# Loading one row of wo per partition in pieces of 69, 48 and 11 partitions, and pairing the exp and transpose tiles, in a cached-attention decode kernel

## The chip, the cores and the metric

The kernel runs on one core of a Trainium2 chip. Of its engines the text names PE (matrix multiplications; PEld is its loading of weights), DVE (vectors), ACT (functions such as exp), POOL and SP, whose queue issues the large loads; 16 DMA engines move the data. A load has landed when its bytes are in the core's memory of 128 partitions. The metric is device microseconds of one execution, lower is better; quoted times are medians over several executions. Executions of one kernel agree within 0.15%, so differences of half a per cent can be told, and "faster" or "slower" needs 2%.

## The reference, cut to what matters

One token goes through two branches that a sigmoid gate mixes. The attention branch has 32 query heads, 4 key/value heads and a cache of 65536 positions, and ends in the projection with `wo`. Inputs are bf16.

```python
q = (x @ wq).reshape(B, Sq, 32, 128).transpose(0, 2, 1, 3)
scores = einsum('bhqd,bhkd->bhqk', q, repeat(k_cache, 8)) * 128 ** -0.5
o = einsum('bhqk,bhkd->bhqd', softmax(scores), repeat(v_cache, 8))
a = o.transpose(0, 2, 1, 3).reshape(B, Sq, 4096) @ wo       # wo is 4096 x 1024
# ... the other branch b: an input projection, gelu, layernorm, an output projection
return g * a + (1 - g) * b
```

The two caches are 64 MB each (4 x 65536 x 128 x 2 bytes), and with the weights 162 MB have to be read once. `wo` is 8 MB of that and is read last.

## The kernel before: the parts that the argument touches

Everything large goes through one buffer `kv` of four slots (4 MB each over 128 partitions), by loads issued on the SP queue. A K tile is transposed on DVE, multiplied on PE, and its scores are copied to an `sc` tile. After the four tiles of a key/value head, `stats` takes the maximum, runs exp on ACT and transposes the result on DVE for the V matmuls:

```python
    def stats(g):
        # ... maximum over the head's four tiles, into nb
        lss[g] = wk.tile([P, NT], FP32, name="ls")
        for j in range(NT):
            nc.scalar.activation(out=sct[g, j][:], in_=sct[g, j][:], func=ACT.Exp, scale=SCALE,
                                 bias=nb[:, 0:1], accum_out=lss[g][:, j:j + 1])
            ptt[g, j] = ptp.tile([P, CC, B], BF16, name="pt")
            nc.vector.transpose(out=ptt[g, j][:].rearrange("p c x -> p (c x)"),
                                in_=sct[g, j][:])
```

The last loads are those of `wo`. A partition holds 32 rows of it (2 KB each): 16 in the first load, then 8, 4, 2, 1 and 1, so that little is left to compute after the last landing:

```python
    wo_view = A_wo.rearrange("(p c) n -> p c n", c=OC)
    c0 = 0
    for at, split in enumerate(WO_SPLIT):              # ((16,), (8, 4, 2, 1, 1))
        for n in split:
            t = load(wo_view[:, c0:c0 + n, :], (n, D), at + c0 % (OC // 2) * D / (CT * P))
            project(t, n, oa, c0, last=(c0 + n == OC))
            c0 += n
```

Of the kernel before, what the change touches and what calls it, by code (L numbers as in the profile page):

```python
# [8 lines left out]
FP32 = mybir.dt.float32  # L9
BF16 = mybir.dt.bfloat16  # L10
I32 = mybir.dt.int32
ACT = mybir.ActivationFunctionType
ALU = mybir.AluOpType
AX = mybir.AxisListType

P = 128
CT = 128
NKV = 4
B = 32
NB = P // B  # L20
VC = 4
CC = CT // VC
ZN = 448
HN = 512
WO_SPLIT = ((16,), (8, 4, 2, 1, 1))


@with_exitstack
def kernel(
# [15 lines left out]
    nc = tc.nc  # L45

    _, _, D = A_x.shape
    _, G, S, DH = A_k_cache.shape
# [7 lines left out]
    OC = HD // P  # L56
    QD = P // H
    NT = S // (P * CT)
# [3 lines left out]
    SCALE = float(DH) ** -0.5  # L62
# [5 lines left out]
    wk = ctx.enter_context(tc.tile_pool(name="wk", bufs=2))  # L68
    big = ctx.enter_context(tc.tile_pool(name="big", bufs=1))
    ktp = ctx.enter_context(tc.tile_pool(name="ktp", bufs=3))  # L70
    scp = ctx.enter_context(tc.tile_pool(name="scp", bufs=NT + 1))
    ptp = ctx.enter_context(tc.tile_pool(name="ptp", bufs=NT + 2))
    pss = ctx.enter_context(tc.tile_pool(name="pss", bufs=2, space=bass.MemoryType.PSUM))
    psm = ctx.enter_context(tc.tile_pool(name="psm", bufs=1, space=bass.MemoryType.PSUM))
    pso = ctx.enter_context(tc.tile_pool(name="pso", bufs=1, space=bass.MemoryType.PSUM))
# [81 lines left out]
    kv = big.tile([P, NKV * CT * P], BF16, name="kv")  # L157

    def load(src, shape, at):
        n = 1  # L160
        for s in shape:
            n *= s
        v = kv[:, int(at * CT * P):int(at * CT * P) + n]
        if len(shape) == 2:
            v = v.rearrange("p (a b) -> p a b", b=shape[1])
        ins = nc.sync.dma_start(out=v, in_=src)  # L166
        if not first_load:
            first_load.append(ins.ins.name)
        return v

    def load_kv(src, g, j, at, n=1):
# [62 lines left out]
    for t in range(2):  # L234
        nc.vector.tensor_tensor(
            out=xm[:, t], in0=xb_ps[:, t * P:(t + 1) * P].rearrange("p (i c) -> p c i", c=KC),
# [51 lines left out]
    for hf in range(2):  # L288
        nc.vector.tensor_tensor(  # L289
            out=zm[:, hf], in0=z_ps[:, hf * HN:hf * HN + ZN].rearrange("p (j c) -> p j c", c=FC),  # L290
# [3 lines left out]
                            in_=zm.rearrange("p h j c -> p h c j"), axis=AX.X, op=ALU.add)  # L294
# [44 lines left out]
    for k in range(NHB):  # L339
# [3 lines left out]
                                                                   j=B, e=2),  # L343
# [29 lines left out]
    late = []  # L373
    sct, ptt, mxs, lss, o_ps = {}, {}, {}, {}, {}

    def k_tile(g, j, kn):
        kb = kn.bitcast(I32)
        n = CC * DH // 2
        s_ps = pss.tile([P, 2 * HN], FP32, name="s_ps", tag="s")
        for v in range(VC):  # L380
            kt = ktp.tile([P, CC * DH], BF16, name="kt")
            nc.vector.transpose(out=kt[:].bitcast(I32), in_=kb[:, v * n:(v + 1) * n])  # L382
            while late:
                nc.vector.reduce_max(**late.pop())  # L384
            kx = kt[:].rearrange("p (c h k e) -> p h e c k", h=2, k=B, e=2)
            for b in range(BP):
                for k in range(2):
                    ins = nc.tensor.matmul(  # L388
                        s_ps[:, k * HN:(k + 1) * HN],
                        lhsT=wt[g % 2][:, v, b].rearrange("p a v h -> p (a v h)"),  # L390
                        rhs=kx[:, b // 2, b % 2, k * CC // 2:(k + 1) * CC // 2, :],
                        start=(v == 0 and b == 0), stop=(v == VC - 1 and b == BP - 1),
                        skip_group_check=True)
                    if k > 0:
                        same_weights(ins)
        if j == 0:
            mxs[g] = wk.tile([P, NT], FP32, name="mx")
        sct[g, j] = scp.tile([P, CC * B], BF16, name="sc")
        nc.scalar.copy(out=sct[g, j][:], in_=s_ps[:])  # L399
        late.append(dict(out=mxs[g][:, j:j + 1], in_=sct[g, j][:], axis=AX.X))  # L400

    def stats(g):
        nc.vector.reduce_max(**late.pop())  # L403
        m1 = wk.tile([P, 1], FP32, name="m1")
        nc.vector.reduce_max(out=m1[:], in_=mxs[g][:], axis=AX.X)  # L405
        mt_ps = psm.tile([1, P], FP32, name="mt_ps", tag="m")
        nc.tensor.transpose(mt_ps[:], m1[:], ident_f[:])  # L407
        gm = wk.tile([1, REP], FP32, name="gm")
        nc.vector.tensor_reduce(out=gm[:], in_=mt_ps[:].rearrange("p (a h) -> p h a", h=REP),
                                axis=AX.X, op=ALU.max)  # L410
        gr = wk.tile([1, P // REP, REP], FP32, name="gr")
        nc.vector.tensor_copy(out=gr[:], in_=gm[:].unsqueeze(1).to_broadcast([1, P // REP, REP]))
        nb_ps = psm.tile([P, 1], FP32, name="nb_ps", tag="m")
        nc.tensor.matmul(nb_ps[:], lhsT=gr[:].rearrange("p a h -> p (a h)"),
                         rhs=ones_f[0:1, 0:1], start=True, stop=True)
        nb = wk.tile([P, 1], FP32, name="nb")
        nc.vector.tensor_scalar(out=nb[:], in0=nb_ps[:], scalar1=-SCALE, scalar2=None,  # L417
                                op0=ALU.mult)
        lss[g] = wk.tile([P, NT], FP32, name="ls")
        for j in range(NT):  # L420
            nc.scalar.activation(out=sct[g, j][:], in_=sct[g, j][:], func=ACT.Exp, scale=SCALE,  # L421
                                 bias=nb[:, 0:1], accum_out=lss[g][:, j:j + 1])
            ptt[g, j] = ptp.tile([P, CC, B], BF16, name="pt")
            nc.vector.transpose(out=ptt[g, j][:].rearrange("p c x -> p (c x)"),  # L424
                                in_=sct[g, j][:])

    def v_tile(g, j, vt):
        if j == 0:
            o_ps[g] = pso.tile([P, 2, VC * DH], FP32, name="o_ps")
        vx = vt.rearrange("p (v c d) -> p c v d", v=VC, d=DH)  # L430
        for u in range(CC // 2):
            hs = slice(u % 2 * P // 2, (u % 2 + 1) * P // 2)
            for e in range(2):
                ins = nc.tensor.matmul(  # L434
                    o_ps[g][hs, e, :],
                    lhsT=ptt[g, j][:, 2 * u:2 * u + 2, :].rearrange("p c x -> p (c x)"),
                    rhs=vx[:, 2 * u + e], start=(j == 0 and u < 2),
                    stop=(j == NT - 1 and u >= CC // 2 - 2), skip_group_check=True)
                if e > 0:
                    same_weights(ins)  # L440

    def head_out(g):
        gs = slice(g * B, (g + 1) * B)
        om8 = big.tile([P, 2 * VC, DH], FP32, name="om8")
        nc.vector.tensor_tensor(  # L445
            out=om8[:], in0=o_ps[g][:].rearrange("p e (v d) -> p (e v) d", d=DH),
            in1=own_8[:].unsqueeze(2).to_broadcast([P, 2 * VC, DH]), op=ALU.mult)
        o_sb = wk.tile([P, DH], FP32, name="o_sb")
        nc.vector.tensor_reduce(out=o_sb[:], in_=om8[:].rearrange("p x d -> p d x"), axis=AX.X,  # L449
                                op=ALU.add)  # L450
        om_ps = psm.tile([P, DH + NT], FP32, name="om_ps", tag="m")
        hs = hsel[:].rearrange("p h q -> p (h q)")
        nc.tensor.matmul(om_ps[gs, DH:], lhsT=hs, rhs=lss[g][:], start=True, stop=True,
                         skip_group_check=True)
        nc.tensor.matmul(om_ps[gs, :DH], lhsT=hs, rhs=o_sb[:], start=True, stop=True,  # L455
                         skip_group_check=True)
        rl = wk.tile([P, 2], FP32, name="rl")
        nc.vector.reduce_sum(out=rl[gs, 0:1], in_=om_ps[gs, DH:], axis=AX.X)
        nc.vector.reciprocal(out=rl[gs, 1:2], in_=rl[gs, 0:1])
        om = wk.tile([P, QD, OC], FP32, name="om")  # L460
        nc.vector.tensor_tensor(
            out=om[gs], in0=om_ps[gs, :DH].rearrange("p (q c) -> p q c", c=OC),
            in1=own_q[gs, :].unsqueeze(2).to_broadcast([B, QD, OC]), op=ALU.mult)
        osum = wk.tile([P, OC], FP32, name="osum")
        nc.vector.tensor_reduce(out=osum[gs, :], in_=om[gs].rearrange("p q c -> p c q"),
                                axis=AX.X, op=ALU.add)
        nc.vector.tensor_scalar(out=oa[gs, :], in0=osum[gs, :], scalar1=rl[gs, 1:2],
                                scalar2=gate[gs, :], op0=ALU.mult, op1=ALU.mult)
# [38 lines left out]
    c0 = 0  # L507
    for at, split in enumerate(WO_SPLIT):
        for n in split:
            t = load(wo_view[:, c0:c0 + n, :], (n, D), at + c0 % (OC // 2) * D / (CT * P))  # L510
            project(t, n, oa, c0, last=(c0 + n == OC))
            c0 += n
    out_sb = const.tile([P, NO], BF16, name="out_sb")
# [45 lines left out]
```

## Time and profile before

| | before |
|---|---|
| median time | 383.88 us (383.83 to 383.91, 3 runs) |
| span of the profiled run | 382.1 us |
| rate of the big loads, from 50 to 370 us | 4 MB every 9.72 us (431 GB/s) |
| last landing of the last V load, of the last `wo` load | 359.68 us, 379.41 us |

The first lines of the page give each engine's busy time and its share of the span; part 3 gives, for each DMA queue, packets, megabytes and the share of the 16 DMA engines' time:

```profile
PE 236.9 (62%) x1372; PEld 60.0 (16%) x796; DVE 218.7 (57%) x211; ACT 39.6 (10%) x55; POOL 4.4 (1%) x10
...
DMA  9999999999999999999999999899999999999995
...
q1 hardware_dynamic: 5188, 162.01, 98.7%
q8 instruction: 8, 0.13, 0.1%
q14 instruction: 3, 0.02, 0.0%
```

The big loads keep the 16 DMA engines busy for 98.7% of the span, and no compute engine passes 62%. So the time is the time of the loads, plus a few microseconds at both ends. Part 3 shows two more queues, with eleven packets: they are instruction fetches.

The end of the chain of waits (start, duration, what):

```profile
340.38 9.32 PE o_ps L434 x64
...
351.51 27.90 DMA kv<-in_A_wo_dram
379.41 0.04 issue
379.45 0.32 PE out_ps L476 x4
```

After 351.51 us there is nothing but waiting for `wo`, and what comes after the landing is short. The exp and the transposes, in the groups part, take a few per cent of two engines that have time to spare (busy us, mean ns | idle before them and its cause):

```profile
L424 DVE STREAM_TRANSPOSE pt<-sc 128x1024 bf16<-128x1024 bf16 x16 | 18.6, 1217 | 6.8 <-ACT sc L421 6.8
...
L421 ACT ACTIVATE sc<-sc,nb 128x1024 bf16<-128x1024 bf16 x16 | 18.2, 1136 | 9.6 <-DVE nb L417 9.6
```

For each load of 128 partitions the trace shows 16 landings, and the page counts 16 DMA engines; a landing is taken as that of one engine's share. For the last `wo` load they were (us):

```
377.34 377.38 377.46 377.55 377.59 377.70 378.21 378.76 378.91 379.01 379.07 379.11 379.13 379.19 379.20 379.41
```

The engines do not end together: six end within 0.4 us, and nine end 1.4 to 2.1 us after the first. The lag has a visible cause. The trace has eight instruction fetches of 16 KB (1.02 to 1.10 us each) and three of 8 KB (0.31 to 0.33 us), and from a fetch on one engine lands later in every load: by about 1.55 us (1.53 to 1.56) after each 16 KB fetch whose engine can be followed, and by 0.7 or 0.97 us after an 8 KB fetch. So a fetch is taken to run on one of the same engines. The spread at the end is what the change is after.

### The profile page before, as it was taken

The page shows a single profiled execution, that of the slowest core. Times are in us where ns is not written, and L with a number is a line of the kernel's source. Part 1 is how long each engine was busy: PE and PEld are TensorE (multiplying, and loading weights), DVE is VectorE, ACT ScalarE, POOL GpSimd, SP SyncE. Part 2 cuts the span into 40 slices and gives each one's busy share as a digit, 9 for nine tenths or more (in the row PEclk, how much of TensorE's full clock was granted, in tenths as well). Part 3 has the DMA queues.
Part 4 walks back from the last instruction along what each step waited for, and adds up shares of the span by engine and source line. Part 5 has one row for each costly group of instructions (what it writes and reads, how often), then busy time and mean ns, then how long its engine had stood idle before and what let it go on. Part 6 is the DMA issues. An engine that isn't in the chain of part 4 may idle for free.

```text
span 382.1 us, 2629 instructions
## 1 busy us (share of the span) xinstructions
PE 236.9 (62%) x1372; PEld 60.0 (16%) x796; DVE 218.7 (57%) x211; ACT 39.6 (10%) x55; POOL 4.4 (1%) x10
## 2 busy tenths in 40 slices
PE   0433457777257966774879485548776964539355
PEld 0110011111111211121112011211111111112123
DVE  4241477997498379555971586659804976400040
ACT  1010001110601101140011011400110105000000
POOL 4000000000000000000000000000000000000000
PEclk9999999998859899867689789897888996959768
DMA  9999999999999999999999999899999999999995
GB/s 379 442 422 418 427 433 439 439 436 428 427 432 429 425 437 453 432 418 418 461 439 394 439 478 439 379 422 463 425 413 432 460 426 425 432 412 427 439 412 221
DMA packets 5239, 162.17 MB, mean 424 GB/s; under 512 B 616, under 2 KB 620, under 8 KB 1004
## 3 DMA queue, kind: packets, MB, share of 16 engines
q1 hardware_dynamic: 5188, 162.01, 98.7%
q8 instruction: 8, 0.13, 0.1%
q14 instruction: 3, 0.02, 0.0%
q10 hardware_dynamic: 40, 0.01, 0.0%
HBM read 162.01 MB, written 0.00 MB: 424 GB/s over the span
## 4 chain that ended last, share of the span: by engine, by line
DMA 57%; PE 22%; DVE 15%; issue 3%; ACT 2%; SPq 0%; DVEq 0%; ACTq 0%
DMA kv<-in_A_v_cache_dram 31%; DMA kv<-in_A_k_cache_dram 14%; DVE kt L382 12%; PE o_ps L434 11%; PE s_ps L388 10%; DMA kv<-in_A_wo_dram 7%; DMA kv<-in_B_w_in_dram 5%; DVE pt L424 1%; ACT sc L399 1%; PE z_ps L275 1%; DVE o_sb L449 0%; SPq L166 0%; ACT L421 0%; ACT sc L421 0%; DVE om L445 0%
## 5 line engine op out<-in xcount | busy, mean ns | idle before, releaser
L388 PE MATMUL s_ps<-kt,wt 128*128 128x512 bf16 x512 | 138.4, 428 | 63.5 <-DVE kt L382 63.3
L382 DVE STREAM_TRANSPOSE kt<-kv 128x2048 int32<-128x2048 int32 x64 | 142.7, 2280 | 39.5 <-DMA kv<-in_A_k_cache_dram 39.5
L434 PE MATMUL o_ps<-kv,pt 128*64 128x512 bf16 x512 | 69.3, 437 | 22.4 <-DMA kv<-in_A_v_cache_dram 22.4
L388 PEld LDWEIGHTS <-wt 128*128 128x128 bf16 x256 | 27.1, 106 | 175.9 <-issue 138.1
L399 ACT CAST sc<-s_ps 128x1024 bf16<-128x1024 f32 x16 | 16.2, 1013 | 245.9 <-PE s_ps L388 245.9
L445 DVE TENSOR_TENSOR om<-o_ps,own 128x1024 f32<-128x1024 f32 x4 | 4.9, 1225 | 46.0 <-PE o_ps L434 46.0
L434 PEld LDWEIGHTS <-pt 128*64 128x64 bf16 x256 | 19.5, 125 | 69.9 <-issue 65.0
L424 DVE STREAM_TRANSPOSE pt<-sc 128x1024 bf16<-128x1024 bf16 x16 | 18.6, 1217 | 6.8 <-ACT sc L421 6.8
L384 DVE TENSOR_REDUCE mx<-sc 128x1 f32<-128x1024 bf16 x12 | 14.5, 1209 | 9.5 <-ACT sc L399 9.4
L421 ACT ACTIVATE sc<-sc,nb 128x1024 bf16<-128x1024 bf16 x16 | 18.2, 1136 | 9.6 <-DVE nb L417 9.6
L403 DVE TENSOR_REDUCE mx<-sc 128x1 f32<-128x1024 bf16 x4 | 4.9, 1220 | 13.6 <-ACT sc L399 13.6
L275 PE MATMUL q_ps<-kv,xT 128*32 128x512 bf16 x64 | 7.2, 630 | 7.3 <-DMA kv<-in_A_wq_dram 7.3
L455 PE MATMUL om_ps<-o_sb,hsel 128*32 128x128 f32 x8 | 2.1, 353 | 12.3 <-DVE o_sb L449 12.3
L275 PE MATMUL z_ps<-kv,xT 128*32 128x448 bf16 x64 | 6.4, 576 | 3.8 <-DMA kv<-in_B_w_in_dram 3.8
L476 PE MATMUL out_ps<-kv,oa 128*32 128x256 bf16 x128 | 6.5, 364 | 3.3 <-DMA kv<-in_A_wo_dram 1.9
L341 DVE TENSOR_TENSOR rowt<-q_ps,own_b 128x512 f32<-128x512 f32 x2 | 1.3, 686 | 12.4 <-PE q_ps L275 12.4
L449 DVE TENSOR_REDUCE o_sb<-om 128x128 f32<-128x1024 f32 x4 | 7.5, 1871 | 0.1
L407 PE MATMUL mt_ps<-ident_f,m 128*1 128x128 f32 x4 | 1.1, 270 | 8.5 <-DVE m L405 8.5
L515 ACT CAST out_sb<-out_ps 128x256 bf16<-128x256 f32 x1 | 0.4, 372 | 56.0 <-PE out_ps L476 56.0
L289 DVE TENSOR_TENSOR rowt<-z_ps,own_b 128x448 f32<-128x448 f32 x2 | 1.2, 618 | 8.6 <-PE z_ps L275 8.6
L275 PEld LDWEIGHTS <-xT 128*32 128x32 bf16 x64 | 3.0, 139 | 19.3 <-issue 19.2
L231 PE MATMUL xb_ps<-xg,spread 8*128 8x256 bf16 x1 | 0.4, 365 | 8.9 <-DMA xg<-in_gate_w_dram 8.9
(88 smaller groups left out, 58.6 us busy)
## 6 DMA issues: line engine op xcount, KB each, us to landing
kv<-in_A_k_cache_dram SPq DMA_DIRECT2D x16, 4096.0 KB, 24.9
kv<-in_A_wq_dram SPq DMA_DIRECT2D x2, 4096.0 KB, 32.7
kv<-in_A_v_cache_dram SPq DMA_DIRECT2D x2, 4096.0 KB
kv<-in_B_w_in_dram SPq DMA_DIRECT2D x2, 3584.0 KB, 18.7
kv<-in_A_wo_dram SPq DMA_DIRECT2D x1, 4096.0 KB
kv<-in_B_w_out_dram SPq DMA_DIRECT2D x1, 3584.0 KB
kv<-in_A_wo_dram SPq DMA_DIRECT2D x1, 2048.0 KB
kv<-in_A_wo_dram SPq DMA_DIRECT2D x1, 1024.0 KB
```

The lines of the kernel that those rows point to most:

```text
L275: ins = nc.tensor.matmul(ps[t * B:(t + 1) * B, k * HN:k * HN + n], lhsT=xT[:, i * KH + c:i * KH + c + 1].to_broadcast([P, B]), rhs=w[:, c, ...
L382: nc.vector.transpose(out=kt[:].bitcast(I32), in_=kb[:, v * n:(v + 1) * n])
L384: nc.vector.reduce_max(**late.pop())
L388: ins = nc.tensor.matmul(s_ps[:, k * HN:(k + 1) * HN], lhsT=wt[g % 2][:, v, b].rearrange("p a v h -> p (a v h)"), rhs=kx[:, b // 2, b % 2, ...
L399: nc.scalar.copy(out=sct[g, j][:], in_=s_ps[:])
L403: nc.vector.reduce_max(**late.pop())
L421: nc.scalar.activation(out=sct[g, j][:], in_=sct[g, j][:], func=ACT.Exp, scale=SCALE, bias=nb[:, 0:1], accum_out=lss[g][:, j:j + 1])
L424: nc.vector.transpose(out=ptt[g, j][:].rearrange("p c x -> p (c x)"), in_=sct[g, j][:])
L434: ins = nc.tensor.matmul(o_ps[g][hs, e, :], lhsT=ptt[g, j][:, 2 * u:2 * u + 2, :].rearrange("p c x -> p (c x)"), rhs=vx[:, 2 * u + e], sta ...
L445: nc.vector.tensor_tensor(out=om8[:], in0=o_ps[g][:].rearrange("p e (v d) -> p (e v) d", d=DH), in1=own_8[:].unsqueeze(2).to_broadcast([P, ...
L449: nc.vector.tensor_reduce(out=o_sb[:], in_=om8[:].rearrange("p x d -> p d x"), axis=AX.X, op=ALU.add)
L476: nc.tensor.matmul(out_ps[t * B:(t + 1) * B, :], lhsT=vec[:, c0 + c:c0 + c + 1].to_broadcast([P, B]), rhs=w[:, c, t * NO:(t + 1) * NO], st ...
```

## The change

Two things, both small. First, of the 16 rows of `wo` that the first load brings to each partition, one leaves it (128 rows, 256 KB in all) and is loaded in three pieces of 69, 48 and 11 partitions. The number of engines that a load uses differs with its partitions. 69 rows go on three engines, and the aim is that engines which would be done early carry more and the others less. Second, exp and the transpose of its result run on two tiles at once, which halves these instructions.

```diff
+WO_PARTS = (69, 48, 11)
...
+    def load_parts(src, parts, at):
+        p0, v = 0, kv[:, int(at * CT * P):int(at * CT * P) + src.shape[1]]
+        for m in parts:
+            nc.sync.dma_start(out=v[p0:p0 + m, :], in_=src[p0:p0 + m, :])
+            p0 += m
+        return v
...
-        for j in range(NT):
-            nc.scalar.activation(out=sct[g, j][:], in_=sct[g, j][:], func=ACT.Exp, scale=SCALE,
-                                 bias=nb[:, 0:1], accum_out=lss[g][:, j:j + 1])
-            ptt[g, j] = ptp.tile([P, CC, B], BF16, name="pt")
-            nc.vector.transpose(out=ptt[g, j][:].rearrange("p c x -> p (c x)"),
-                                in_=sct[g, j][:])
+        for h in range(NT // 2):
+            sc = sct[g, h][:].rearrange("p t x -> p (t x)")
+            nc.scalar.activation(out=sc, in_=sc, func=ACT.Exp, scale=SCALE,
+                                 bias=nb[:, 0:1], accum_out=lss[g][:, h:h + 1])
+            ptt[g, h] = ptp.tile([P, 2 * CC, B], BF16, name="pt")
+            nc.vector.transpose(out=ptt[g, h][:].rearrange("p c x -> p (c x)"), in_=sc)
...
-            t = load(wo_view[:, c0:c0 + n, :], (n, D), at + c0 % (OC // 2) * D / (CT * P))
+            r = at + c0 % (OC // 2) * D / (CT * P)
+            if c0 == 0:
+                load(wo_view[:, 1:n, :], (n - 1, D), r + D / (CT * P))
+                load_parts(wo_view[:, 0, :], WO_PARTS, r)
+                t = kv[:, at * CT * P:at * CT * P + n * D].rearrange("p (c n) -> p c n", n=D)
+            else:
+                t = load(wo_view[:, c0:c0 + n, :], (n, D), r)
```

More of the change, by code (lines that the diff above doesn't have):

```diff
@@ L70 @@
     ktp = ctx.enter_context(tc.tile_pool(name="ktp", bufs=3))
-    scp = ctx.enter_context(tc.tile_pool(name="scp", bufs=NT + 1))
-    ptp = ctx.enter_context(tc.tile_pool(name="ptp", bufs=NT + 2))
+    scp = ctx.enter_context(tc.tile_pool(name="scp", bufs=NT // 2 + 1))
+    ptp = ctx.enter_context(tc.tile_pool(name="ptp", bufs=NT // 2 + 1))
     pss = ctx.enter_context(tc.tile_pool(name="pss", bufs=2, space=bass.MemoryType.PSUM))
@@ L397, in k_tile @@
             mxs[g] = wk.tile([P, NT], FP32, name="mx")
-        sct[g, j] = scp.tile([P, CC * B], BF16, name="sc")
-        nc.scalar.copy(out=sct[g, j][:], in_=s_ps[:])
-        late.append(dict(out=mxs[g][:, j:j + 1], in_=sct[g, j][:], axis=AX.X))
+        if (g, j // 2) not in sct:
+            sct[g, j // 2] = scp.tile([P, 2, CC * B], BF16, name="sc")
+        sc = sct[g, j // 2][:, j % 2]
+        nc.scalar.copy(out=sc, in_=s_ps[:])
+        late.append(dict(out=mxs[g][:, j:j + 1], in_=sc, axis=AX.X))
     def stats(g):
@@ L418, in stats @@
                                 op0=ALU.mult)
-        lss[g] = wk.tile([P, NT], FP32, name="ls")
-        for j in range(NT):
-            nc.scalar.activation(out=sct[g, j][:], in_=sct[g, j][:], func=ACT.Exp, scale=SCALE,
-                                 bias=nb[:, 0:1], accum_out=lss[g][:, j:j + 1])
-            ptt[g, j] = ptp.tile([P, CC, B], BF16, name="pt")
-            nc.vector.transpose(out=ptt[g, j][:].rearrange("p c x -> p (c x)"),
-                                in_=sct[g, j][:])
+        lss[g] = wk.tile([P, NT // 2], FP32, name="ls")
+        for h in range(NT // 2):
[4 more added lines that the diff above has]
+            nc.vector.transpose(out=ptt[g, h][:].rearrange("p c x -> p (c x)"), in_=sc)
     def v_tile(g, j, vt):
@@ L432, in v_tile @@
             hs = slice(u % 2 * P // 2, (u % 2 + 1) * P // 2)
+            c0 = j % 2 * CC + 2 * u
             for e in range(2):
@@ L435, in v_tile @@
                     o_ps[g][hs, e, :],
-                    lhsT=ptt[g, j][:, 2 * u:2 * u + 2, :].rearrange("p c x -> p (c x)"),
+                    lhsT=ptt[g, j // 2][:, c0:c0 + 2, :].rearrange("p c x -> p (c x)"),
                     rhs=vx[:, 2 * u + e], start=(j == 0 and u < 2),
@@ L450, in head_out @@
                                 op=ALU.add)
-        om_ps = psm.tile([P, DH + NT], FP32, name="om_ps", tag="m")
+        om_ps = psm.tile([P, DH + NT // 2], FP32, name="om_ps", tag="m")
         hs = hsel[:].rearrange("p h q -> p (h q)")
```

## The prediction

> **What bounds the kernel now.** The DMA engines, from end to end. The page's DMA queue line has the big loads at 98.7% of 16 engines' span; no compute engine is over 62%. The semaphore landings in the trace show 4 MB every 9.72 us (431 GB/s) without a break from 49.97 to 369.41 us, so the last-landing engine never waits for an issue. In the queue's own waits SP waits often, but each time with at least one load (some 9 us) still in flight.
>
> **What is left to gain.** The 16 engines do not end together. Their last wo landings spread over 2.07 us: six lie within 0.37 us, one at 0.88 and nine from 1.4 to 2.07. The trace shows why: queue 8 fetches 16 KB of instructions eight times (1.05 to 1.1 us each) and queue 14 fetches 8 KB three times (0.32 us), each on one DMA engine, and after each one engine's landings come 0.7 to 1.55 us later for good. The two 8 KB fetches at 50.4 and 220.0 us hit the same engine, which is the last (2.07). The one at 308.9 comes when ACT nears its 64th instruction.
>
> **The wo row.** [...] A 2 KB packet takes 84 ns, and 2 KB within a 32 KB packet 76 ns (1216 ns / 16). [...] If 1 and 2 are early, they end near 1.75 to 1.9 and the last other engine at 1.75 to 1.8: the end moves 0.2 to 0.3 us. Three more issues on SP cost about 0.45 us each at 350 us, hidden: 18 us of loads are queued then.
>
> **Exp and transpose in pairs.** ACT has eight exp (1136 ns) and eight accumulator reads fewer, DVE eight transposes (1217 ns) fewer; an estimate from these and the 2280 ns of the 2048-word K transpose is 0.3 us less DVE work a group. The first transpose of a group starts some 1.1 us later, as it waits for a double exp. All of that has 9 us of slack. What may count is that ACT then has 62 instructions instead of 78, so its fetch at 308.9 should vanish and that engine ends 0.7 us earlier. SP's three more could bring a fetch of its own near 352 us, which would take the gain back if it hits a late engine.
>
> **Time.** 383.9 - 0.25 = 383.6 us; range 383.0 to 384.3. Same: 98 in 100.
>
> **What would show it.** Last landings: spread under 1.4 us instead of 2.07, the last 0.2 to 0.4 us earlier against the 369.41 landing's pace; eight exp and eight transposes of twice the size (near 2.0 and 2.3 us); two 8 KB fetches, or three with one near 352 us; the 4 MB cadence unchanged.
>
> **What would make it wrong.** Engine 1 or 2 being a late one (+1.5 us); [...] shifting rows frees nothing; a fetch moved to another engine.

The cut passages of "The wo row" said which engines carry which rows of the three pieces, and what each gains or loses by it; no trace shows that, as a packet in it does not name its engine. The sum came to an end 0.2 to 0.3 us earlier, and 0.25 of that stands in 383.9 - 0.25 = 383.6 us. Its terms were estimates from 84 ns for a 2 KB packet and 76 ns for 2 KB within a larger one: 0.25 us gained by eight engines, 0.34 by five, and 1.65 lost by three. The 1 and 2 that are named there are two of these three engines; that they are early is a condition, and their end near 1.75 to 1.9 us is an estimate too.

## The result, and the profile after

| | before | after |
|---|---|---|
| median time | 383.92 us (383.83 to 384.00, 6 runs) | 385.48 us (385.31 to 385.66, 6 runs) |
| ratio to before | | 1.0041 (1.0028 to 1.0054) |
| span of the profiled run | 382.1 us | 383.7 us |
| last landing of the last V load | 359.68 us | 359.54 us |
| last landing of the last `wo` load | 379.41 us | 380.73 us |

Ratios here and below are the mean time of one kernel's runs over that of the other's of the same rounds, so not quite the ratio of the medians quoted. The change is slower by 1.6 us, where 0.3 us faster was predicted. By the 2% bar it is "the same", but the measured time is outside the predicted range, and the sign is wrong.

The lines of the page that answer to those of before:

```profile
PE 236.5 (62%) x1372; PEld 60.7 (16%) x796; DVE 218.2 (57%) x203; ACT 37.3 (10%) x39; POOL 4.4 (1%) x10
...
q1 hardware_dynamic: 5346, 162.01, 98.7%
q8 instruction: 8, 0.13, 0.1%
q14 instruction: 2, 0.02, 0.0%
...
L435 DVE STREAM_TRANSPOSE pt<-sc 128x2048 bf16<-128x2048 bf16 x8 | 18.0, 2291 | 10.2 <-ACT sc L432 10.2
...
L432 ACT ACTIVATE sc<-sc,nb 128x2048 bf16<-128x2048 bf16 x8 | 15.9, 1994 | 9.9 <-DVE nb L427 9.9
```

The pairs did what they were to do: half as many instructions, a little less busy time, and one instruction fetch fewer on queue 14. DVE waits 3.4 us more for exp (10.2 against 6.8), and that costs nothing, as the last V load lands 0.14 us earlier than before.

So the time was lost between 359.54 us and the end: 21.19 us for `wo` (380.73 - 359.54) instead of 19.73. The end of the chain of waits names nothing but `wo`:

```profile
346.37 23.38 DMA kv<-in_A_wo_dram
369.75 0.02 issue
369.76 10.97 DMA kv<-in_A_wo_dram
380.73 0.04 issue
380.77 0.43 PE out_ps L487 x3
```

The stretches view gives each window's engine times and, at the end of the line, granted clock, DMA share and GB/s (it counts a packet where it starts, so 5 us are rough). First before, then after:

```profile
356.00:366.00 10.00, 6.28 (x32) 1.69 (x15) 0.00 (x0) 0.00 (x0) 0.00 (x0) 0.66 1.01 436
366.00:371.00 5.00, 0.93 (x6) 0.32 (x4) 3.99 (x6) 0.00 (x0) 0.00 (x0) 0.78 0.95 406
371.00:376.00 5.00, 4.61 (x96) 3.58 (x97) 0.30 (x1) 0.00 (x0) 0.00 (x0) 0.54 0.96 398
```

```profile
356.00:366.00 10.00, 5.13 (x34) 1.49 (x17) 1.37 (x2) 0.00 (x0) 0.00 (x0) 0.83 1.02 434
366.00:371.00 5.00, 0.41 (x2) 0.14 (x2) 2.92 (x6) 0.00 (x0) 0.00 (x0) 0.82 0.93 269
371.00:376.00 5.00, 3.91 (x72) 3.17 (x76) 0.00 (x0) 0.00 (x0) 0.00 (x0) 0.50 0.98 408
```

The DMA share stays above 0.9 while the rate falls to two thirds: the engines are as busy as before and move less. Each packet's bytes, spread evenly over its duration, give the rate by the microsecond:

| from, us | 366 | 367 | 368 | 369 | 370 |
|---|---|---|---|---|---|
| before, GB/s | 431 | 430 | 428 | 429 | 428 |
| after, GB/s | 372 | 297 | 287 | 231 | 330 |

The five differences add up to 629 KB not moved (59 + 133 + 141 + 198 + 98), which at 430 GB/s is 1.46 us: all of the loss in `wo` (21.19 - 19.73). The packets of that stretch show it one by one. The 128 packets of the split row (2 KB; in the last loads of before such a packet took 84 to 96 ns, 86 on average) took 127 ns on average and up to 204. The 16 KB packets that began from 360 to 372 us took 787 ns on average and up to 1215 (before: 616 and 621). The last 30 KB packets took up to 1681, where 1139 to 1148 is the usual. For the last load the 16 landings were:

```
378.52 378.56 378.66 378.97 380.08 380.20 380.22 380.22 380.28 380.29 380.34 380.38 380.38 380.40 380.48 380.73
```

Four engines are early instead of six or seven, and all 16 are later, the early ones too. Rows were shifted, but something slowed every engine while it happened.

### The profile page after: what moved, and what is told of

It is laid out like the page before. It is cut to its first block, busy times and chain, and to the rows that moved or that the text cites. A ratio compares the mean times of both kernels' runs of the same rounds, so it can differ in the third digit from the quotient of the medians.

```text
span 383.7 us, 2603 instructions
## 1 busy us (share of the span) xinstructions
PE 236.5 (62%) x1372; PEld 60.7 (16%) x796; DVE 218.2 (57%) x203; ACT 37.3 (10%) x39; POOL 4.4 (1%) x10
## 4 chain that ended last, share of the span: by engine, by line
DMA 58%; PE 21%; DVE 15%; issue 3%; ACT 2%; DVEq 0%; ACTq 0%
DMA kv<-in_A_v_cache_dram 30%; DMA kv<-in_A_k_cache_dram 14%; DVE kt L390 12%; PE o_ps L445 10%; PE s_ps L396 10%; DMA kv<-in_A_wo_dram 9%; DMA kv<-in_B_w_in_dram 5%; DVE pt L435 1%; ACT sc L409 1%; PE z_ps L283 1%; ACT sc L432 1%; DVE o_sb L460 0%; ACT L432 0%; DVE om L456 0%; DVE mx L413 0%
## 5 line engine op out<-in xcount | busy, mean ns | idle before, releaser
L445 PE MATMUL o_ps<-kv,pt 128*64 128x512 bf16 x512 | 67.0, 427 | 20.5 <-DMA kv<-in_A_v_cache_dram 20.3
L435 DVE STREAM_TRANSPOSE pt<-sc 128x2048 bf16<-128x2048 bf16 x8 | 18.0, 2291 | 10.2 <-ACT sc L432 10.2
L432 ACT ACTIVATE sc<-sc,nb 128x2048 bf16<-128x2048 bf16 x8 | 15.9, 1994 | 9.9 <-DVE nb L427 9.9
L487 PE MATMUL out_ps<-kv,oa 128*32 128x256 bf16 x128 | 8.0, 415 | 5.0 <-DMA kv<-in_A_wo_dram 5.0
L487 PEld LDWEIGHTS <-oa 128*32 128x32 bf16 x128 | 5.4, 137 | 7.6 <-issue 6.8
```

The lines of the kernel that those rows point to most:

```text
L432: nc.scalar.activation(out=sc, in_=sc, func=ACT.Exp, scale=SCALE, bias=nb[:, 0:1], accum_out=lss[g][:, h:h + 1])
L435: nc.vector.transpose(out=ptt[g, h][:].rearrange("p c x -> p (c x)"), in_=sc)
L445: ins = nc.tensor.matmul(o_ps[g][hs, e, :], lhsT=ptt[g, j // 2][:, c0:c0 + 2, :].rearrange("p c x -> p (c x)"), rhs=vx[:, 2 * u + e], star ...
L487: nc.tensor.matmul(out_ps[t * B:(t + 1) * B, :], lhsT=vec[:, c0 + c:c0 + c + 1].to_broadcast([P, B]), rhs=w[:, c, t * NO:(t + 1) * NO], st ...
```

## The experiments

The theory after this, a guess to be tested: an engine that writes into partitions which another engine's stream is writing at that time shares a path with it, and both slow down. Which engine writes which partitions no trace shows. What they show fits eight packets per engine in a big load: 128 packets of 32 KB and 1216 ns on 16 engines make 8 x 1.216 = 9.73 us, and 4 MB take 9.72. An engine's own partitions are, here and below, the eight that it writes in such a load, taken to be the same eight in each (not shown). The piece of 69 has three landings, so about 23 rows to an engine (an estimate, 69/3), and then most of them lie in partitions of other engines. The rivals: the pairs of exp and transpose; the small packets; the uneven load of the engines; the HBM side, where rows of `wo` are 64 KB apart.

All results in one table. Runs of a letter share a chip and its runs of before. "wo" is the last landing of `wo` minus that of the last V load (before: 19.73).

| run | chip | time, us | of before, us | ratio (95%) | wo, us |
|---|---|---|---|---|---|
| rows_only | A | 386.33 | 384.00 | 1.0060 (1.0047 to 1.0072) | 22.02 |
| pairs_only | A | 384.18 | 384.00 | 1.0005 (0.9991 to 1.0019) | 19.73 |
| parts128 | A | 384.20 | 384.00 | 1.0007 (0.9995 to 1.0020) | 19.78 |
| parts64 | A | 385.54 | 384.00 | 1.0040 (1.0027 to 1.0052) | 21.03 |
| again | B | 385.47 | 383.99 | 1.0039 (1.0027 to 1.0052) | 20.96 |
| pitch62 | B | 385.47 | 383.99 | 1.0039 (1.0026 to 1.0051) | 20.85 |
| alternate | B | 384.33 | 383.99 | 1.0007 (0.9995 to 1.0020) | 19.80 |
| parts16 | B | 385.50 | 383.99 | 1.0041 (1.0027 to 1.0054) | 20.74 |
| probe_spread | C | 385.10 | 383.97 | 1.0029 (1.0014 to 1.0044) | 20.67 |
| probe_crowd | C | 387.69 | 383.97 | 1.0095 (1.0080 to 1.0111) | 22.79 |
| probe_cross | C | 386.87 | 383.97 | 1.0075 (1.0058 to 1.0092) | 22.40 |

### Which half of the change

rows_only is the kernel before with `load_parts` and the split row of the diff above, and nothing else of it. pairs_only is the change with the old line for `wo`:

```diff
-            r = at + c0 % (OC // 2) * D / (CT * P)
-            if c0 == 0:
-                load(wo_view[:, 1:n, :], (n - 1, D), r + D / (CT * P))
-                load_parts(wo_view[:, 0, :], WO_PARTS, r)
-                t = kv[:, at * CT * P:at * CT * P + n * D].rearrange("p (c n) -> p c n", n=D)
-            else:
-                t = load(wo_view[:, c0:c0 + n, :], (n, D), r)
+            t = load(wo_view[:, c0:c0 + n, :], (n, D), at + c0 % (OC // 2) * D / (CT * P))
```

> The kernel before, with the row of wo split over 69, 48 and 11 partitions and nothing else of the change. Theory (the row split costs it, because engines write into partitions that other engines' streams are writing, and all slow down): the whole loss is here, 385.3 to 385.7 us, and 2 KB packets and their neighbours near 366 to 371 us last up to twice as long as elsewhere. Rival (the pairs of exp and transpose cost it, by delaying the V stage or a fetch of instructions): 383.9 or a little less.

> The change with wo loaded as before, so the pairs alone. Theory: off the critical path, 383.7 to 384.0 us, one 8 KB instruction fetch fewer (two instead of three). Rival (the pairs cost it): 385.0 or more.

The row costs it; the pairs alone are as before within the interval (384.18 us, a little above the 383.7 to 384.0 that were expected). The stretches view, rows_only first, then pairs_only:

```profile
366.00:371.00 5.00, 0.90 (x6) 0.32 (x4) 3.98 (x6) 0.00 (x0) 0.00 (x0) 0.78 0.94 262
```

```profile
366.00:371.00 5.00, 1.11 (x8) 0.32 (x4) 3.81 (x6) 0.00 (x0) 0.00 (x0) 0.81 0.95 406
```

rows_only came out 0.8 us worse than the whole change (0.0021 of 384 us), which was not expected. Its trace has one engine that finishes alone, at 381.62 us, 0.62 us after the one before it. rows_only still has the third 8 KB fetch, at 308.9 us, and the whole change has not. An engine that is set back by a fetch (0.7 us by this one) and then gets 27 rows (an estimate from the landings of the three pieces: 69/3 + 48/16 + 11/11) would look like that: the pairs, which drop the fetch, would then be what makes the split less costly. That is argued from the times; a packet in the trace does not name its engine.

### Small packets, or where they are written

Both are the change with another constant:

```diff
-WO_PARTS = (69, 48, 11)
+WO_PARTS = (128,)          # parts128
+WO_PARTS = (64, 64)        # parts64
```

> The change with the row in one piece of 128 partitions: the same extra small packets (2 KB, 64 KB apart in HBM), each engine 8 rows as in the big loads, no shift of bytes between engines. Theory (writing out of the engine's own partitions): as before, 383.7 to 384.2 us, 2 KB packets near 84 ns. Rival (small packets or strided reads beside the large ones, whoever writes them): most of the loss stays, 385 us or more.

> The change with the row as 64 and 64 partitions[...]. Theory (writes outside an engine's own partitions share a write path): slower than the one piece by 0.5 us or more, 2 KB packets near twice 84 ns. Rival (the uneven load, [...] costs it): as the one piece of 128, 383.7 to 384.2 us.

With 128 partitions the same row, in the same 2 KB packets, costs nothing: 85 ns a packet on average and at most 93. With 64 and 64 the load should be even too: pieces of 48 and of 128 partitions show 16 landings, and four rows per engine and piece are the author's estimate from that (no landings were counted for 64). Yet 1.3 us are lost, nearly all that the whole change loses, and `wo` takes 1.25 us more than with the row in one piece (21.03 against 19.78). If the estimate holds, the uneven load is not what costs most of it: 1.30 of the 1.46 us are lost without it. The stretches view, parts128 first, then parts64:

```profile
366.00:371.00 5.00, 0.84 (x18) 0.57 (x22) 3.87 (x7) 0.00 (x0) 0.00 (x0) 0.99 0.96 402
```

```profile
366.00:371.00 5.00, 1.09 (x8) 0.32 (x4) 3.83 (x6) 0.00 (x0) 0.00 (x0) 0.81 0.93 294
```

The 2 KB packets of parts64 took 112 ns on average and up to 180, where near twice 84 had been expected, and 16 KB packets up to 1273.

### The HBM side, and how crowded the partitions are

again is the whole change unaltered. pitch62 reads the split row from wrong rows (so its result is not the right one), 62 KB apart instead of 64. alternate and parts16 change only which partitions go together:

```diff
 # pitch62
+    wo_62 = A_wo[:(OC - 1) * P, :].rearrange("(p c) n -> p c n", c=OC - 1)
-                load_parts(wo_view[:, 0, :], WO_PARTS, r)
+                load_parts(wo_62[:, 0, :], WO_PARTS, r)
 # alternate: even partitions, then odd ones
-        for m in parts:
-            nc.sync.dma_start(out=v[p0:p0 + m, :], in_=src[p0:p0 + m, :])
-            p0 += m
+        for p0 in range(2):
+            nc.sync.dma_start(out=v[p0:P:2, :], in_=src[p0:P:2, :])
 # parts16
-WO_PARTS = (69, 48, 11)
+WO_PARTS = (16, 16, 32, 64)
```

> The whole change again, unaltered, so that the other three have it on the same chip: 385.3 to 385.7 us, against 384.0 of before.

> The whole change, but the split row is read from rows 62 KB apart in HBM instead of 64 KB (the wrong rows, so a wrong result on purpose); partitions, packets and engines are unaltered. Theory (the SBUF side: several engines write into the same partitions' path): as the whole change, 385.3 to 385.7 us, 2 KB packets still up to 200 ns. Rival (the HBM side: rows a power of two apart meet in one place of the memory): 384.0 to 384.3 us, 2 KB packets back to 84 ns.

> As the 64 and 64 partitions, but the even partitions in one piece and the odd in the other: [...] each piece reaches over all 128 partitions instead of one half. Theory in its narrow form (16 engines crowd on the write paths of half the partitions, and those of the other half lie idle): near the one piece of 128, 384.2 to 384.6 us. Wide form (any write outside an engine's own partitions costs): near the two halves, 385.2 us or more. HBM theory: as the two halves, as the reads are as many and as far apart or more.

> The row as 16, 16, 32 and 64 partitions: [...] a quarter of them goes to 16 partitions at a time, an eighth of all. Theory (crowding on the partitions' write paths): slower than the two halves of 64, 385.8 us or more, with 2 KB packets to 300 ns. Rival (uneven load of the engines, or the mere number of pieces): near 384.2 to 384.5 us.

The HBM side is out as the pitch goes: the same time to 0.01 us, and 2 KB packets of 125 ns on average and up to 195 (again: 126 and 185).

alternate has the same number of pieces and rows per piece as parts64 (and of rows per engine, if the estimate there holds for both), and loses nothing: 85 ns a packet, at most 89. So a piece that was spread over all 128 partitions was free (1.0007), and one that was confined to half of them was not (1.0040). The stretches view of alternate, to set beside that of parts64:

```profile
366.00:371.00 5.00, 1.61 (x26) 1.09 (x30) 3.11 (x7) 0.00 (x0) 0.00 (x0) 0.83 0.95 396
```

parts16 is a miss. It was to be worse than parts64, and is not (20.74 us for `wo` against 21.03, on another chip), and no 2 KB packet took more than 169 ns. In the two pieces of 16 each engine would have just one packet (an estimate; their landings were not counted), and the engines, whose landings lie 2.07 us apart in before, would reach it at different times, so few of them can have met there. That explanation is argued. By it the experiment was too weak a dose, and the next one repeats it with larger packets.

### The disputed cost by itself

The kernel is pairs_only, plus three loads of 8 KB to each of 8 partitions of a spare buffer that nobody reads; the result stays right. They stand where the row was split. Only the slice differs:

```diff
             t = load(wo_view[:, c0:c0 + n, :], (n, D), at + c0 % (OC // 2) * D / (CT * P))
+            if c0 == 0:
+                for k in range(3):
+                    spare = ktp.tile([P, CC * DH], BF16, name="spare", tag="kt")
+                    nc.sync.dma_start(
+                        out=spare[0:32:4, :].rearrange("p (c n) -> p c n", n=D),   # probe_spread
+                        in_=wo_view[0:32:4, 4 * k:4 * k + 4, :])
+                    # probe_crowd has 0:8 in both places, probe_cross 64:96:4
```

> The pairs alone, and beside them, at the place where the row was split, three loads of 8 KB to each of 8 partitions of a spare buffer that nobody reads [...]. Here the partitions are 0, 4, 8, ... 28, one in each group of four. [...] If these are the engines' own partitions, the packets take 310 to 330 ns, the neighbours are not slowed, and the time is 384.2 plus at most 0.95, so 384.4 to 385.2 us.

> The same loads to partitions 0 to 7, so eight engines write into two groups of four partitions. If partitions in groups of four share a write path (theory A), the 8 KB packets take 500 ns or more, [...] and the run is 0.5 us or more above the spread one. If only writes that cross from one half of the partitions to the other cost (theory B), 310 to 330 ns and the time of the spread one within 0.2 us.

> The same loads to partitions 64, 68, ... 92, spread as in the first, but in the upper half. [...] 8 KB packets up to twice 313 ns, and 16 and 32 KB packets of others up to a half longer. If no engine has partitions of its own (rival C: only how many engines write at one place counts), as the spread one.

The 0.95 us of the first are three packets of 313 ns on one engine: an estimate, as the two loads of 8 partitions in before (x and the gate's weights) show eight landings each, so that 24 packets would make three on each of eight engines. The longer packets of the third are what theories A and B give, on the supposition that the probe's engines have their own partitions in the lower half; that was not shown. Nor were the groups of four in theory A: they are a supposition of it.

The 24 packets of each probe, in the order in which they started, took (ns):

```
probe_spread  309 309 309 315 316 309 315 315 309 312 309 309 309 311 315 316 309 316 316 311 309 309 311 315
probe_crowd   309 309 309 393 309 480 721 431 516 971 1018 625 636 996 955 362 335 320 441 435 784 633 940 632
probe_cross   309 309 316 309 366 475 488 533 565 614 632 612 613 632 604 365 351 345 391 649 425 585 620 593
```

The spread probe adds 0.94 us to `wo` (20.67 - 19.73), which is three packets (3 x 313 ns), those of one engine by the estimate above; nothing is left for a slowing of others, and its own packets took 316 ns at most. The same bytes crowded into eight neighbouring partitions take up to 1018 ns a packet and cost 3.06 us (22.79 - 19.73). Spread over partitions 64, 68, ... 92, they take 488 ns on average and up to 649, about the twice 313 that the theory gives for two streams on one path, and cost 2.67 us. The neighbours fared worse than expected: 16 KB packets took up to 1229 ns, twice their usual time (616), where half as long again was the most foreseen. Theory A fits both, though no run tests the size of its groups: partitions 0, 4, ... 28 in one load take 309 to 316 ns for 8 KB, partitions 0 to 7 up to 1018. Theory B, that only crossing to the other half costs, falls with the crowd probe: its partitions lie in the same half as those of the spread probe, and it cost 3.06 us against 0.94. Rival C falls with probe_cross, which is as spread as probe_spread and cost 2.67 us. One rival is not separated from theory A: except in pitch62, the rows of `wo` that an engine reads move along with the partitions that it writes. A matter of pitch it is not, as probe_spread and probe_cross both read rows 256 KB apart, and pitch62, which moves the rows by up to 254 KB (127 x 2 KB) and leaves the partitions, lost as much. But no run keeps the rows and moves the partitions alone. The stretches view of the three, in this order:

```profile
366.00:371.00 5.00, 0.83 (x6) 0.29 (x4) 4.06 (x7) 0.00 (x0) 0.00 (x0) 0.76 0.91 387
```

```profile
366.00:371.00 5.00, 0.84 (x10) 0.34 (x14) 3.88 (x7) 0.00 (x0) 0.00 (x0) 0.66 1.05 272
```

```profile
366.00:371.00 5.00, 0.42 (x6) 0.25 (x8) 3.68 (x7) 0.00 (x0) 0.00 (x0) 0.96 1.00 285
```

The probes also show why a small detour costs so much. The crowd probe writes into eight partitions, yet the whole core loses nearly half its rate: 224 GB/s from 368 to 369 us, where spread has 427. In that microsecond 17 packets of 16 KB or more were under way, and the fastest took 1.6 times as long as it does undisturbed. At each instant of it 11 to 14 such packets were in flight. If the probe is on eight engines only, as estimated above, and an engine has one such packet in flight at a time, then three or more of these engines carry nothing of the probe, and they are held up too. That is argued from the counts, not shown by name.

One thing stays open. alternate loses nothing, and which engine writes which of its partitions was not shown. Either its rows fall to the engines that own them, or two short packets on one path do no harm, and then theory A is too wide as it stands. The packets do not show which. No version beat both kernels: pairs_only and parts128 are as before. Nor can the theory give one by another choice of parts, since by it a row carried by another engine goes through the owner's path; that is argued, not run.

## Why the prediction was wrong

- **The gain of 0.25 us for eight engines and 0.34 us for five: wrong, and this is the step that failed.** The prediction costed a shifted row at 84 ns, what a 2 KB packet takes at the least in the last loads of before (86 on average), which cover all 128 partitions, and took the rest of the stream as undisturbed. The shifted rows took 127 ns on average, and the 16 KB packets around them 787 instead of 616. In place of 0.25 us gained, 1.46 us were lost in `wo` (21.19 - 19.73).
- **"Shifting rows frees nothing": named as a risk, and undersized.** The prediction saw that freeing nothing was possible. That the detour would cost all 16 engines was not seen.
- **The number of engines by partitions (3, 16 and 11): right.** The three pieces show 3, 16 and 11 landings in the trace, from 367.32 us on. Two lone increments of their semaphores, at 347.22 and 348.05 us, come soon after the issues and are not counted among them.
- **Engines 1 and 2 early: consistent with the landings, not shown by name.** At 357 us eight engines are early and eight late. Three early ones given more rows, and one hit by the fetch at 374.9 us, leave four, and four are early at the end. It did not help.
- **"Spread under 1.4 us instead of 2.07": wrong.** 2.21 us (378.52 to 380.73).
- **The pairs off the critical path, ACT's fetch gone, no new one near 352 us: right.** Queue 14 has two fetches instead of three, and pairs_only is at 1.0005. That the lost fetch was ACT's is argued from the counts, not shown: 63 of ACT's 78 instructions had started at 308.9 us, and after the change the trace has 56 in all, where 62 were expected. Exp took 1994 ns and the transpose 2291, where near 2000 and 2300 were expected. The estimate of 0.3 us less DVE work a group was too high: 0.15 us (18.6 - 18.0 over four groups).
- **The cadence of 4 MB every 9.72 us unchanged up to `wo`: right.** The last V load lands at 359.54 us, against 359.68.

## What to carry to other kernels

Where loads bind, look at which partitions they write and not only at the bytes per engine. Here the row cost nothing when it was loaded over all 128 partitions, in one piece or as the even and the odd ones (1.0007 both), and it cost 1.3 to 1.5 us of `wo` when its pieces were of 64 and 64 partitions, or of 69, 48 and 11 (21.03 and 21.19 against 19.73); so load over all 128, and do not move rows to another engine by picking other partition counts. A DMA share near 1 with GB/s that has dropped was the sign of such crowding here (0.93 at 269 GB/s, where before had 0.95 at 406); look at single packets' durations, and test with a spare load to spread and to crowded partitions. Halving instructions on engines with slack was worth no time here (pairs_only, 1.0005), although it saved 2.3 us of ACT's busy time.
